# Moving the last two query casts later and cutting them in quarters, with a fourth pair of strips

## The chip, the cores and the metric

The kernel runs on one core of one Trainium2 chip. The core has five instruction queues that run side by side and wait for each other through semaphores: PE (TensorE, matrix products and transposes; its weight loads are shown as PEld), DVE (VectorE), ACT (ScalarE), POOL (GpSimd) and SP (SyncE, which here only issues transfers). Transfers are carried out by 16 DMA engines; a transfer issued on SP's queue appears as q1 in the profile, one issued on POOL's queue as q0.

The metric is the device time of one launch in microseconds (us). The kernel before took 377.2 us in the median of three runs (375.63 to 378.17). Its profile is that of another execution, which took 375.06 us.

## The reference, cut to what matters

Two parts follow each other. The first is attention whose keys and values are one small projected table per batch; the second sends each row of its result through two of eight small adapters.

```python
B, N, C = q.shape                      # 4, 12288, 128
kv_pool = kv.reshape(B, H//4, 4, W//4, 4, C).mean(axis=(2, 4))
k = v = kv_pool.reshape(B, -1, C) @ w_sr          # 768 rows a batch
a = softmax(q @ k.T / sqrt(C))                    # 12288 x 768 a batch
x = (a @ v).reshape(B * N, C)                     # 49152 rows
logits = x @ w_gate                               # 8 experts
w = softmax of the two largest logits
out = x + sum over those two e of w_e * (x @ A[e]) @ B[e]     # rank 16
```

## The kernel before, in words

The 49152 rows are cut into 96 chunks of 512 rows (`T`), numbered k = 0 to 95; four chunks make a query group g of 2048 rows (`GT`), 24 groups in all, six to a batch. The main loop has one slot per chunk number. In slot k the scores of a later chunk are computed (`scores`: PE tile `sg`, exponentials on ACT into `em`), chunk k-1 is attended (`attend`: PE tile `acc`), and older chunks go through the adapter steps: `normalize` (DVE, `xn`), a transposition of `xn`, `down` (PE, `h_ps`), `gate` (DVE, multiplies `h_ps` by the gates `gw`), a transposition of the gated activations, `up` (PE, `d_ps`), `finish` (DVE, `osb`) and a store of `osb` to the output. `route` and `gates` work out the gates on POOL. The order on each engine is the order in which the loop records the operations; nothing reorders them.

**Queries.** Groups 2 and up come in two steps. `cast_q` (L79 to L84) issues on POOL's queue a transfer from the float32 queries to a bf16 buffer in device memory, `qbf`, laid out in 16 rows of eight pieces of 2048 elements. `load_qT` and `part_qT` (L86 to L92) later issue on SP's queue a transposing transfer from `qbf` to the tile `qT`. The tables `casts` and `loads` (L492 to L496) say in which slot: the casts of groups 4 to 23 stand in slots 8, 12, 15, 18 and so on to 66, always first in the slot (`begin`); the loads of the last groups stand in slots 61, 64, 67, 74, 78, 82 and 86. From slot 72 on a load is cut in two halves, two slots apart. Groups 0 and 1 are loaded as float32 (`load_q`, L109) and transposed by PE instead; their eight tiles `qf` are taken from the pool of `osb`.

**Transpositions by transfer.** In slots 13 to 69 about three gated chunks in four are transposed by a transfer: `gate_turn` writes the gated activations into one half of a strip `hs` and a transfer on SP's queue turns it into a strip `ht`; two chunks share one pair of strips. There are three `hs` and four `ht`, used in turn, so that a gate that opens a new pair waits until the transfers from the pair three before it have landed. The chunk goes through `up` six slots after its gate. From slot 70 on, another form is used: `narrow` (L415, POOL) writes the normalized chunk of the slot as bf16 into a strip `turn`, `gate` writes the gated chunk beside it, and one transfer (`turn_dma`, L419) turns both. Chunks 68 to 89 (`by_dma`) have their normalized rows turned so; the product `h_ps` of slot k+2 reads what the transfer of slot k has brought.

**SP's queue** issues in program order: loads of kv rows, stores, `ht` transfers, `qT` loads, `turn` transfers. One that cannot be issued yet holds those behind it.

**The output pool** `opool` has six buffers `osb`; the one that writes the seventh waits until the store from the first has landed.

The lines that the steps below touch, in `begin` and `gate_turn`:

```python
if k in casts:
    cast_q(4 + casts.index(k))
...
sheets.append([hpool.tile([P, 2, S, P], BF16, tag=tag, name=tag, bufs=n)
               for tag, n in (("hs", 3), ("ht", 4))])
```

Of the kernel before, what the change touches and what calls it, by code (L numbers as in the profile page):

```python
# [10 lines left out]
FP32 = mybir.dt.float32  # L11
BF16 = mybir.dt.bfloat16
# [8 lines left out]
def kernel(  # L21
# [10 lines left out]
    nc = tc.nc  # L32
    P = 128
    B, N, C = q.tensor.shape
# [5 lines left out]
    S = T // P  # L40
    GC = 4
    GT = GC * T
# [15 lines left out]
    gpool = ctx.enter_context(tc.tile_pool(name="gpool", bufs=6))  # L58
    run = ctx.enter_context(tc.tile_pool(name="run", bufs=3))
    hpool = ctx.enter_context(tc.tile_pool(name="hpool", bufs=4))  # L60
    opool = ctx.enter_context(tc.tile_pool(name="opool", bufs=6))
    qdram = ctx.enter_context(tc.tile_pool(name="qdram", bufs=1, space=bass.MemoryType.DRAM))
    ps_s = ctx.enter_context(tc.tile_pool(name="ps_s", bufs=2, space=bass.MemoryType.PSUM))
    ps_a = ctx.enter_context(tc.tile_pool(name="ps_a", bufs=1, space=bass.MemoryType.PSUM))
# [2 lines left out]
    keep = tc.keep_in_program_order  # L67
# [8 lines left out]
    NG = N // GT  # L76
    q_bf, qT, kvr, spare = {}, {}, {}, {}

    def cast_q(g):  # L79
        t = qdram.tile([16, GT // 16 * C], BF16, tag=f"q{g}", name=f"qbf{g}")  # L80
        src = q[g // NG, (g % NG) * GT:(g % NG + 1) * GT]
        keep(nc.gpsimd.dma_start(t.rearrange("r (u x) -> r u x", u=8),
                                 src.rearrange("(u r x) c -> r u (x c)", r=16, u=8)))
        q_bf[g] = t  # L84

    def load_qT(g):  # L86
        qT[g] = qpool.tile([P, GT], BF16, tag="qT", name="qT")
# [7 lines left out]
    def load_kv(b, h, r, x):  # L95

        if (b, h) not in kvr:
            kvr[b, h] = kvpool.tile([P, 4, 2, 4 * C], FP32, tag="kvr", name="kvr")
        rows = H // 3
        src = kv[b, h * rows + r:(h + 1) * rows:4].rearrange("y (w k) c -> y w (k c)", k=8)  # L100
        if x is None:
            keep(nc.sync.dma_start(kvr[b, h][:, r].rearrange("p g c -> p (g c)"), src))
        else:
            keep(nc.sync.dma_start(kvr[b, h][:, r, x], src[:, :, x * 4 * C:(x + 1) * 4 * C]))


    q_f = {}

    def load_q(g, m):  # L109
        q_f[g, m] = opool.tile([P, S, C], FP32, tag="osb", name="qf")  # L110
        src = q[0, g * GT:(g + 1) * GT].rearrange("(p j) c -> p j c", p=P)
        keep(nc.sync.dma_start(q_f[g, m], src[:, m * S:(m + 1) * S]))

# [44 lines left out]
    for m in range(GC):  # L158
        load_q(0, m)
    load_first(1)  # L160
    load_first(2)
    for m in range(GC):
        load_q(1, m)
# [174 lines left out]
    SOLO, TURN = NCHUNK - 6, NCHUNK - 28  # L338
# [91 lines left out]
    def gate(k, into=None):  # L430
        k0, m = first[k], k - first[k]
        hg[k] = run.tile([P, S, P], BF16, tag="hg", name="hg") if into is None else into
        keep(nc.vector.tensor_tensor(  # L433
            hg[k].rearrange("p s (e r) -> p (s e) r", e=E),
            hp[k].rearrange("p s (e r) -> p (s e) r", e=E),
            gw[k0][:, m * S:(m + 1) * S].rearrange("p s e -> p (s e)")
            .unsqueeze(2).broadcast_to([P, S * E, RK]), op=ALU.mult))

    sheets, turns = [], []

    def gate_turn(k, alone):
        i = len(turns) % 2
        if i == 0:
            sheets.append([hpool.tile([P, 2, S, P], BF16, tag=tag, name=tag, bufs=n)
                           for tag, n in (("hs", 3), ("ht", 4))])
        src, dst = sheets[-1]
        gate(k, src[:, i])
        hgT[k] = dst[:, i]
        turns.append(k)
        if alone or i == 1:  # L450
            lo = i if alone else 0
            keep(nc.sync.dma_start(dst[:, lo:i + 1].rearrange("c h s p -> c (h s) p"),
                                   src[:, lo:i + 1].rearrange("p h s c -> p (h s c)"), transpose=True))
# [26 lines left out]
    def cast_first():  # L480
        keep(nc.gpsimd.tensor_copy(late, q_f[1, 2][:, 0, 0:1]))
        for g in (2, 3):
            cast_q(g)
        for g in (2, 3):
            load_qT(g)
# [5 lines left out]
        scores(k, r)  # L491

    sums, rest = [], []
    casts = [8, 12] + [15 + 3 * i for i in range(18)]
    loads = {4 * g - 6: g for g in range(4, B * NG) if not 17 <= g <= 19}
    loads.update({61: 17, 64: 18, 67: 19})  # L496
    assert len(casts) == B * NG - 4

    rows_at, adds_at = {}, {}
    for b in range(2, B):  # L500
        for n in range(12):
            h, r, t = n // 4, n % 4, b * NB - 33 + 2 * n
# [15 lines left out]
    def begin(k):  # L518
        nonlocal sums, rest
        b, i = divmod(k, NB)  # L520
        g = k // GC
        if k in casts:
            cast_q(4 + casts.index(k))
        if k in rows_at:
            load_kv(*rows_at[k], None)
        if i == 0 and 0 < b < B - 1:
            rest = prepare(b + 1, nc.gpsimd)[1]
        if k == 3:
            sums, rest = prepare(1, nc.gpsimd)
            sums = sum(sums, [])  # L530
        if 3 <= k < 15:
            load_kv(1, (k - 3) // 4, (k - 3) % 4, None)
        if k == 7:
            for _ in range(2):
                sums.pop(0)()
# [11 lines left out]
    enter, t, left = {}, 1, list(range(NCHUNK - 3))  # L547
# [14 lines left out]
    def step(op, *w):  # L562
        v = [int(x) if x.isdigit() else engines.get(x, pools.get(x)) for x in w]
        if op == "T":
            turn_rows(v[0], 2 * (v[2] // 2) if w[1] == "s" else v[2],
                      v[2] % 2 if w[1] == "s" else v[3])
        elif op == "turn":
            turn_q(v[0] // GC, v[0] % GC, *v[1:])
        elif op in ("keys", "keys2", "values"):
            first_rest[v[0]][("keys", "keys2", "values").index(op)]()  # L570
        elif op == "gates":
            later.pop(0)()
        else:
            {"spin": spin, "proj1": project, "proj2": project2, "sum": add_rows, "sc": unit,
             "late": cast_first, "cast": cast_weights, "slot": begin, "at": attend, "atp": attend_part,
             "norm": normalize, "top": top, "route": route, "tr": transposes, "down": down,
             "gate": gate, "up": up, "fin": finish}[op](*v)
# [23 lines left out]
    for k in range(k1, NCHUNK):  # L601
        b, i = divmod(k, NB)
        ka = att.get(k, [])
        kx = enter.get(k, [])
        begin(k)

        def after_norm(kn):
# [86 lines left out]
        for x_ in kx[:1]:  # L694
            if x_ in by_queue:
                gate_turn(x_, x_ < 59 or x_ == TURN - 3)
                late_up[k + 6] = [x_]
                if k in loads:
                    load_qT(loads[k])
            elif x_ in by_strip:  # L700
                gate(x_, strip(k, 0)[:, 1])
                turn_dma(k, *todo, (hgT, x_))
                todo = []
            else:
                gate(x_)
# [200 lines left out]
```

## Time and profile before

| what | us |
|---|---|
| median of three runs | 377.2 |
| the profiled execution | 375.06 |
| its span, first to last instruction | 373.2 |
| PE busy (96% of the span) | 359.1 |
| ACT busy (79%) | 295.2 |
| DVE busy (78%) | 291.3 |
| POOL busy (58%) | 218.2 |
| DMA, q1 (SP's queue), share of 16 engines | 78.2% |
| DMA, q0 (POOL's queue: the casts), share of 16 engines | 18.2% |

A row of the timeline gives start, duration, engine, line, operation, out<-in, shapes and count; brackets behind it give how long the engine had been idle and what ended that. SP's rows are durations of issuing; when the data lands is told apart from that ("DMA to landing"). A wait is put down to the semaphore that moved last, so where the engine named had long been done the true releaser was another one, often a transfer. The shares of the queues are sums over packets, each from its start to its end, and can pass 100%.

### The profile page before, as it was taken

Reading aid. Unit: us, or ns where it says so; the run is one execution under the profiler, and the core shown is the slowest. Engines: PE = TensorE matmul, PEld = TensorE weight load, DVE = VectorE, ACT = ScalarE, POOL = GpSimd, SP = SyncE. Lnnn points to the kernel's source line nnn. Section 1 sums busy time; section 2 is a strip of 40 time slices with the busy share of each in tenths; the row PEclk is TensorE's granted clock in tenths of the full one; section 3 lists DMA queues with packets and bytes.
Section 4 is the critical chain, followed back from the end, with each engine's and each line's share of the span. In section 5 each row is a group of like instructions: output and inputs, shape, how many; then the busy total and the mean of one; then the engine's idle time right before and its main releaser. Section 6 shows DMA issues by size and latency. Waiting matters only on the chain.

```text
span 373.2 us, 11208 instructions
## 1 busy us (share of the span) xinstructions
PE 359.1 (96%) x4254; PEld 280.5 (75%) x4260; DVE 291.3 (78%) x924; ACT 295.2 (79%) x368; POOL 218.2 (58%) x493
## 2 busy tenths in 40 slices
PE   8799999999999999999999999999898999999993
PEld 5577778877787787787787777777676777777782
DVE  1446789887888888888888898888687877777785
ACT  1448986777778888888888888878777999999873
POOL 0120368888766566667657657658454666666452
PEclk9999999999999999999999999999999999999998
DMA  7989669999999999999899999999999999999523
GB/s 250 383 289 227 227 162 295 287 255 241 200 249 321 262 245 227 275 265 290 223 237 217 229 264 249 308 230 223 238 235 191 257 201 222 201 222 201 142 89 141
DMA packets 77222, 88.36 MB, mean 237 GB/s; under 512 B 53584, under 2 KB 54352, under 8 KB 76752
## 3 DMA queue, kind: packets, MB, share of 16 engines
q1 hardware_dynamic: 73568, 75.91, 78.2%
q0 software_dynamic: 3168, 11.54, 18.2%
q8 instruction: 33, 0.54, 0.6%
q10 hardware_dynamic: 432, 0.20, 0.2%
q14 instruction: 21, 0.17, 0.1%
HBM read 50.53 MB, written 36.70 MB: 234 GB/s over the span
## 4 chain that ended last, share of the span: by engine, by line
PE 85%; DMA 6%; DVE 3%; ACT 2%; POOL 1%; issue 1%; SPq 0%; ACTq 0%; POOLq 0%; DVEq 0%
PE acc L70 34%; PE sg L70 30%; PE h_ps L70 5%; PE tt_ps L70 5%; PE d_ps L70 5%; DMA kvr<-in_kv_dram 4%; PE kpT_ps L70 2%; DMA turn<-turn 2%; PE v_ps L70 1%; ACT em L303 1%; DVE xn L332 1%; DVE kvr L135 1%; POOL kvr L221 1%; DMA out_dram<-osb 1%; PE kfT_ps L70 1%
## 5 line engine op out<-in xcount | busy, mean ns | idle before, releaser
L303 ACT ACTIVATE em<-sg 128x1024 f16<-128x1024 f32 x288 | 284.2, 1022 | 59.4 <-PE sg L70 53.0
L70 PE MATMUL sg<-qT,kfT 128*128 128x512 bf16 x570 | 169.5, 379 | 1.0 <-ACT em L303 0.7
L70 PE MATMUL acc<-vx,em 128*128 128x136 f16 x2280 | 167.2, 223 | 0.6 <-DVE xn L332 0.5
L70 PEld LDWEIGHTS <-em 128*128 128x128 f16 x2304 | 146.7, 98 | 18.2 <-DVE xn L332 2.4
L332 DVE TENSOR_TENSOR xn<-acc,rinv 128x540 f32<-128x540 f32 x95 | 68.4, 720 | 3.3
L466 DVE TENSOR_TENSOR osb<-d_ps,xn 128x512 f32<-128x512 f32 x91 | 62.1, 687 | 1.8
L364 POOL TENSOR_TENSOR over<-xn,srt 128x64 f32<-128x64 f32 (+1 forms) x120 | 30.9, 278 | 49.7 <-DVE srt L352 49.7
L516 POOL TENSOR_TENSOR kvr<-kvr 128x512 f32<-128x512 f32 (+1 forms) x48 | 57.0, 1202 | 0.5
L70 PEld LDWEIGHTS <-kfT 128*128 128x128 bf16 x576 | 45.1, 98 | 2.7 <-issue 1.0
L379 POOL TENSOR_TENSOR gw<-th,over 128x64 f32<-128x64 f32 (+1 forms) x60 | 17.3, 289 | 50.8 <-ACT th L377 48.6
L324 DVE RECIPROCAL rinv<-acc 128x4 f32<-128x4 f32 x95 | 17.3, 182 | 37.5 <-PE acc L70 35.0
L433 DVE TENSOR_TENSOR hs<-h_ps,gw 128x512 bf16<-128x512 f32 x45 | 30.6, 679 | 7.5 <-POOL gw L380 4.9
L401 DVE COPY tts<-tt_ps 128x512 bf16<-128x512 bf16 (+1 forms) x72 | 35.8, 497 | 0.0
L70 PEld LDWEIGHTS <-xn 128*128 128x128 bf16 x296 | 22.5, 98 | 16.7 <-DVE xn L332 0.4
L352 DVE MAX8 srt<-xn 128x8 f32<-128x8 f32 x380 | 34.4, 152 | 0.1
L70 PEld LDWEIGHTS <-tts 128*128 128x128 bf16 x376 | 26.1, 98 | 5.9 <-DVE tts L401 0.2
L70 PE MATMUL h_ps<-a_bf,tts 128*128 128x128 bf16 x284 | 27.5, 219 | 0.0
L70 PE MATMUL tt_ps<-id_bf,xn 128*128 128x128 bf16 x284 | 27.4, 219 | 0.0
L70 PEld LDWEIGHTS <-turn 128*128 128x128 bf16 x184 | 13.8, 98 | 12.9 <-DMA turn<-turn 3.6
L370 POOL TENSOR_SCALAR over<-over 128x64 f32<-128x64 f32 (+1 forms) x60 | 19.8, 331 | 5.3
L223 POOL TENSOR_TENSOR kvr<-kvr 128x512 f32<-128x512 f32 x18 | 22.4, 1270 | 0.1
L70 PEld LDWEIGHTS <-ht 128*128 128x128 bf16 x180 | 13.8, 98 | 10.9 <-issue 0.7
(96 smaller groups left out, 295.9 us busy)
## 6 DMA issues: line engine op xcount, KB each, us to landing
out_dram<-osb SPq DMA_DIRECT2D x94, 256.0 KB, 4.8
kvr<-in_kv_dram SPq DMA_DIRECT2D x45, 512.0 KB, 6.7
qbf<-in_q_dram POOLq DMA_DIRECT2D x22, 512.0 KB, 7.2
qf<-in_q_dram SPq DMA_DIRECT2D x8, 256.0 KB, 7.6
kvr<-in_kv_dram SPq DMA_DIRECT2D x6, 256.0 KB, 7.7
ht<-hs SPq DMA_TRANSPOSE x42, 6.4
qT<-qbf SPq DMA_TRANSPOSE x26, 7.7
out_dram<-osb SPq DMA_DIRECT2D x3, 128.0 KB, 2.3
```

The source lines that it names most:

```text
L70: return keep(nc.tensor.matmul(*a, **k))
L223: keep(adder.tensor_tensor(u[:, lo:hi], u[:, lo:hi], v[:, lo:hi], op=ALU.add))
L303: keep(nc.scalar.activation(o, i_, AF.Exp, bias=0.0, scale=scale))
L324: keep(nc.vector.reciprocal(ri, acc[k][:, :, VC]))
L332: keep(nc.vector.tensor_tensor(x[:, :, 0:VC], acc[k][:, :, 0:VC], ri.unsqueeze(2).broadcast_to([P, S, VC]), op=ALU.mult))
L352: keep(nc.vector.max(srt[k0][:, m, s], xn[k][:, s, C:C + E]))
L364: keep(eng.tensor_tensor(d, lg, so[:, :, i].unsqueeze(2).broadcast_to([P, n, 8]), op=ALU.subtract))
L370: keep(eng.tensor_scalar(mask, mask, 0.0, None, op0=ALU.is_ge))
L401: keep(nc.vector.tensor_copy(sb[:, lo:hi], ps[:, lo:hi]))
L433: keep(nc.vector.tensor_tensor(hg[k].rearrange("p s (e r) -> p (s e) r", e=E), hp[k].rearrange("p s (e r) -> p (s e) r", e=E), gw[k0][:, m ...
L466: keep(nc.vector.tensor_tensor(osb, dp[k], xn[k][:, :, 0:C], op=ALU.add))
L516: keep(nc.gpsimd.tensor_tensor(u, u, v, op=ALU.add))
```

## The change

Four things change.

1. The casts of groups 22 and 23 leave slots 63 and 66. Each is cut in four by rows of `qbf` (rows 0 to 3, 4 to 7, 8 to 11, 12 to 15); the quarters of group 22 stand first in slots 72, 73, 74 and 75, those of group 23 in slots 78, 79, 80 and 81. A whole cast reads 16 x 8 pieces of 2048 elements, a quarter 4 x 8.
2. The strips `hs` become four, as the strips `ht` are.
3. The four `qf` tiles of group 1 are taken from the strips `ht`, reread as float32, not from the pool of `osb`.
4. The pool of `osb` has five buffers instead of six.

```diff
-    opool = ctx.enter_context(tc.tile_pool(name="opool", bufs=6))
+    opool = ctx.enter_context(tc.tile_pool(name="opool", bufs=5))
...
-    def cast_q(g):
-        t = qdram.tile([16, GT // 16 * C], BF16, tag=f"q{g}", name=f"qbf{g}")
+    def cast_q(g, lo=0, hi=16):
+        if lo == 0:
+            q_bf[g] = qdram.tile([16, GT // 16 * C], BF16, tag=f"q{g}", name=f"qbf{g}")
         src = q[g // NG, (g % NG) * GT:(g % NG + 1) * GT]
-        keep(nc.gpsimd.dma_start(t.rearrange("r (u x) -> r u x", u=8),
-                                 src.rearrange("(u r x) c -> r u (x c)", r=16, u=8)))
-        q_bf[g] = t
+        keep(nc.gpsimd.dma_start(q_bf[g].rearrange("r (u x) -> r u x", u=8)[lo:hi],
+                                 src.rearrange("(u r x) c -> r u (x c)", r=16, u=8)[lo:hi]))
...
     def load_q(g, m):
-        q_f[g, m] = opool.tile([P, S, C], FP32, tag="osb", name="qf")
+        if g:
+            t = hpool.tile([P, 2, S, P], BF16, tag="ht", name="qf")
+            q_f[g, m] = t.rearrange("p h s c -> p (h s c)").bitcast(FP32).rearrange("p (s c) -> p s c", s=S)
+        else:
+            q_f[g, m] = opool.tile([P, S, C], FP32, tag="osb", name="qf")
...
-            sheets.append([hpool.tile([P, 2, S, P], BF16, tag=tag, name=tag, bufs=n)
-                           for tag, n in (("hs", 3), ("ht", 4))])
+            sheets.append([hpool.tile([P, 2, S, P], BF16, tag=tag, name=tag)
+                           for tag in ("hs", "ht")])
...
-    casts = [8, 12] + [15 + 3 * i for i in range(18)]
+    casts = [8, 12] + [15 + 3 * i for i in range(16)]
+    quarters = {TURN + 4 + 6 * n + i: (B * NG - 2 + n, 4 * i) for n in range(2) for i in range(4)}
...
         if k in casts:
             cast_q(4 + casts.index(k))
+        if k in quarters:
+            g, r = quarters[k]
+            cast_q(g, r, r + 4)
```

More of the change, by code (lines that the diff above doesn't have):

```diff
@@ L493 @@
     sums, rest = [], []
-    casts = [8, 12] + [15 + 3 * i for i in range(18)]
+    casts = [8, 12] + [15 + 3 * i for i in range(16)]
+    quarters = {TURN + 4 + 6 * n + i: (B * NG - 2 + n, 4 * i) for n in range(2) for i in range(4)}
     loads = {4 * g - 6: g for g in range(4, B * NG) if not 17 <= g <= 19}
     loads.update({61: 17, 64: 18, 67: 19})
-    assert len(casts) == B * NG - 4
+    assert len(casts) == B * NG - 6
     rows_at, adds_at = {}, {}
```

## The prediction

> **What bounds the kernel now.** I read the busy shares, then the table of stretches, to see where PE loses time.
>
> ```profile
> PE 359.1 (96%) x4254; PEld 280.5 (75%) x4260; DVE 291.3 (78%) x924; ACT 295.2 (79%) x368; POOL 218.2 (58%) x493
> ```
> ```profile
> 250.00:260.00 10.00, 10.00 (x123) 7.70 (x122) 7.84 (x26) 8.73 (x11) 6.61 (x13) 1.00 1.16 227
> 260.00:270.00 10.00, 8.79 (x106) 6.65 (x105) 7.09 (x22) 7.25 (x10) 5.44 (x10) 1.00 1.07 232
> 270.00:280.00 10.00, 9.88 (x118) 7.58 (x114) 8.40 (x30) 7.66 (x11) 5.40 (x18) 1.00 1.06 233
> 280.00:290.00 10.00, 8.59 (x106) 6.77 (x107) 7.44 (x21) 7.72 (x11) 5.03 (x17) 1.00 0.89 190
> ```
>
> PE is busy 96% of the span, and a stretch in which it is full gives nothing back. In these rows (start and end, length, then busy time of PE, PEld, DVE, ACT and POOL) PE has a hole of 1.21 us in 260 to 270 and of 1.53 in 270 to 290. The timeline says what made them.
>
> ```profile
> 261.93 0.36 DVE L352 MAX8 srt<-xn 128x8 f32<-128x8 f32 x4
> 264.45 0.69 DVE L433 TENSOR_TENSOR hs<-h_ps,gw 128x512 bf16<-128x512 f32 x1 [2.16 <-PE sg L70]
> 265.19 0.38 PE L70 MATMUL d_ps<-b_bf,ht 128*128 128x128 bf16 x4 [0.75 <-DVE hs L433]
> 266.04 0.53 PE L70 MATMUL acc<-vx,em 128*128 128x136 f16 x6 [0.47 <-DVE xn L332]
> ```
> ```profile
> 281.41 0.40 PE L70 MATMUL h_ps<-a_bf,turn 128*128 128x128 bf16 x4 [1.53 <-DMA turn<-turn]
> ```
>
> The first hole is a gate on DVE that stood idle for 2.16 us before it wrote `hs`. PE `sg` is named as its releaser, but this gate (chunk 63) reads no scores; it opens a new pair of strips, and with three pairs it needs the one of chunks 57 and 58 back. PE waits for the gate (0.75) and then for the late `xn` behind it (0.47). The second hole, 1.53 us before 281.41, stands ahead of the first product that reads a `turn` strip.
>
> ```profile
> 246.74 1.22 SPq L452 DMA_TRANSPOSE ht<-hs  x1
> 247.61 0.60 POOL L82 DMA_DIRECT2D qbf<-in_q_dram  x1
> 256.96 0.60 POOL L82 DMA_DIRECT2D qbf<-in_q_dram  x1
> 250.65 6.51 SPq L92 DMA_TRANSPOSE qT<-qbf  x1
> 257.87 1.54 SPq L452 DMA_TRANSPOSE ht<-hs  x1
> 261.65 5.42 SPq L92 DMA_TRANSPOSE qT<-qbf  x1
> 270.45 2.72 SPq L92 DMA_TRANSPOSE qT<-qbf  x1
> 274.82 0.69 DVE L433 TENSOR_TENSOR turn<-h_ps,gw 128x512 bf16<-128x512 f32 x1 [0.55 <-POOL gw L380]
> 278.23 1.29 SPq L419 DMA_TRANSPOSE turn<-turn  x1
> ```
>
> Both holes come from SP's queue running late. The two `qT` loads issued beside the casts of slots 63 and 66 took 6.51 and 5.42 us to issue, the next one, with no cast, 2.72. Chunk 58's transfer stood behind the first of them and was issued at 257.87. The first `turn` strip was written at 275.51, its transfer issued only at 278.23.
>
> What a cast does to the other queue stands in the DMA view: the stretch of the cast at 256.96 (rows q0 and q1: packets, MB, share of 16 engines), then a stretch with none.
>
> ```profile
> q0 software_dynamic: 144, 0.52, 57.0%
> q1 hardware_dynamic: 652, 0.39, 23.2%
> ```
> ```profile
> q1 hardware_dynamic: 4899, 2.57, 107.7%
> ```
>
> 57.0% of the 6.7 us from 256.9 to 263.6 is 3.8 us of each engine for the cast; meanwhile SP's queue falls to 23.2%, against 107.7% from 301 to 313. The landings agree: the `ht` transfer of 257.87 (first row below), and that of 276.28 with no cast near.
>
> ```profile
> DMA to landing us min/median/max: 6.5/6.5/6.5
> ```
> ```profile
> DMA to landing us min/median/max: 3.1/3.1/3.1
> ```
>
> So a whole cast adds up to 3.4 us to a transfer beside it.
>
> **The change part by part.** *Casts leave slots 63 and 66.* The two `qT` loads fall towards 2.72 us, which gives SP back (6.51 - 2.72) + (5.42 - 2.72) = 6.5 us, more than the 2.7 us by which the first `turn` transfer was late. Issued at 275.5 and landing 3.1 later it is there at 278.6, before the 279.88 at which PE wanted it: gain 1.53.
>
> *Fourth pair.* Chunk 63's gate then needs the pair before that of 57 and 58, whose last transfer is that of 246.74; and with SP earlier chunk 58's transfer lands earlier as well, which matters, since the product at 265.19 reads it. Gain 0.75 + 0.47 = 1.22. Together 2.75, all that PE loses between 250 and 290. The other gates hide their waits in slack already; DVE finds nothing later behind it.
>
> *Five output buffers.* This is the page's row of the stores (KB each, median us to landing):
>
> ```profile
> out_dram<-osb SPq DMA_DIRECT2D x94, 256.0 KB, 4.8
> ```
>
> One `osb` is written a slot, and a slot is 3.2 us or more (304.81 to 307.98 below), so five buffers leave about 16 us for a store that lands in 4.8: nothing. In the tail the last write reuses, instead of the buffer of chunk 91's store, that of chunk 92's, issued at 367.64:
>
> ```profile
> 367.64 2.60 SPq L462 DMA_DIRECT2D out_dram<-osb  x5
> 369.46 0.42 DVE L776 TENSOR_TENSOR osb<-tail_ps,xn 128x256 f32<-128x256 f32 x1 [0.36 <-PE tail_ps L70]
> ```
> ```profile
> DMA to landing us min/median/max: 2.0/2.0/2.0
> ```
>
> It lands at 369.66, the write began at 369.46: loss 0.2 on the path that ends the kernel. The end of the run hangs on this write and its store, so nothing hides it.
>
> *First loads.* Two of the `qf` tiles of group 1 no longer wait until PE has read those of group 0. SP's list of waits has this for them:
>
> ```profile
> SPq L112 <- DMA kvr<-in_kv_dram: 2.2, 4, 0.9
> ```
>
> They waited for kv transfers, not for PE, and that order stays: zero.
>
> *Quarters on POOL.* Each costs 0.60 us of issue (the rows above), eight of them 4.8. In their slots POOL has this gap:
>
> ```profile
> 301.62 0.29 POOL L370 TENSOR_SCALAR over<-over 128x32 f32<-128x32 f32 x1
> 302.43 0.61 POOL L415 CAST turn<-xn 128x512 bf16<-128x512 f32 x1 [0.52 <-DVE xn L332]
> ```
>
> The quarter stands between these two: 301.91 + 0.60 = 302.51, so `narrow` is 0.1 late at most, and its transfer, issued at 303.26, still finds it done at 303.12. Zero; up to 0.1 a slot if that cover goes.
>
> *Quarters beside the `turn` transfers.* This decides the sign. The transfer of slot k needs the gate of slot k, and the product `h_ps` of slot k+2 needs the transfer: a loop over two slots.
>
> ```profile
> 303.26 1.30 SPq L419 DMA_TRANSPOSE turn<-turn  x1
> 306.93 1.52 SPq L419 DMA_TRANSPOSE turn<-turn  x1
> 304.81 0.39 PE L70 MATMUL h_ps<-a_bf,turn 128*128 128x128 bf16 x4
> 307.98 0.39 PE L70 MATMUL h_ps<-a_bf,turn 128*128 128x128 bf16 x4
> 311.42 0.40 PE L70 MATMUL h_ps<-a_bf,turn 128*128 128x128 bf16 x4
> DMA to landing us min/median/max: 3.4/4.1/4.4
> ```
> ```profile
> 286.22 2.24 SPq L419 DMA_TRANSPOSE turn<-turn  x1
> 291.82 0.39 PE L70 MATMUL h_ps<-a_bf,turn 128*128 128x128 bf16 x4
> DMA to landing us min/median/max: 3.5/3.6/3.8
> ```
>
> The landing rows are for the four transfers of 301 to 311, slots 77 to 80, and the three of 286 to 294, slots 73 to 75. In slots 78 and 79 there lie 4.72 and 4.49 us between issue and product, mean 4.6; less the median landing of 4.1 the slack is 0.5. In slots 72 to 75, where PE does more per slot, it is 5.6 - 3.6 = 2.0. A delay d that lasts stretches two slots by d less the slack, one slot by half of that.
>
> No row shows a quarter, so d has two ends. Spread over all 16 engines like a whole cast, a quarter takes 3.8 / 4 = 0.95 us of each: d is at most 0.95. But only 4 rows of 8 pieces are read now instead of 16; if the 16 rows were what filled the 16 engines, four engines get what each got from a whole cast, 3.8 us, and a transfer that uses all engines lands when the slowest is done. A slot is 3.2 us, so the delay saturates there: d = 3.2. I take 2.0, the middle, because the two ends are equally near to the one kind of row there is. Slots 78 to 81 then cost 4 x (2.0 - 0.5) / 2 = 3.0, slots 72 to 75 nothing.
>
> The sum: -2.75 + 0.2 + 3.0 = +0.45 us. On its own execution 375.06 becomes 375.5; the median of the runs is 2.1 above that execution, so I carry the difference over: 377.2 becomes 377.6, no change.
>
> [...]
>
> **The rivals.** *The quarters spread evenly* (faster). d = 0.95 costs 4 x 0.45 / 2 = 0.9: -2.75 + 0.2 + 0.9 = -1.65, 375.5; with no cost at all 374.6. For it: 16 engines carry every transfer seen. Against: those had 16 or more outer rows.
>
> *Each quarter holds four engines as long as a whole cast held all* (slower). d = 3.2 costs 4 x 2.7 / 2 = 5.4 in slots 78 to 81 and 4 x 1.2 / 2 = 2.4 in slots 72 to 75: +7.8 + 0.2 - 2.75 = +5.25, 382.4. It outweighs the gain from d = 1.8 and passes 1% from d = 2.8. For it: the 3.4 us that a whole cast added to a transfer. Against: slots that get longer move the transfers away from the next quarter.
>
> *The change does not do what it says*: SP stays late from its kv loads and stores alone, and the first `turn` transfer with it. Only the 1.22 comes: +2.0, 379.2. Against: the 2.72 row.
>
> **How the numbers follow.** Forecast 0.38 (376.4 to 379), even spread 0.30, slower rival 0.20, SP still late 0.12. Below 374.6 and above 382.4 I leave about one in ten each. A difference under 1%, 3.8 us, is about what a measurement of this kernel cannot tell from no change. Faster by over 1% would need more than the 2.75 there is to gain: 0.05. Slower by over 1% is the slower rival: 0.20. The rest, 0.75, lies within.
>
> **What would show it.** After the change the gate of chunk 63 has no idle time before it and PE no hole between 260 and 282, with `qT` loads near 2.7 us; if they still take 5, the first step is wrong. In slots 78 to 81 the waits of PE `h_ps` for `turn` give 2(d - 0.5) in total; none means an even spread, about 5 us the slower rival. Holes in slots 72 to 75 speak for d over 2. The last write of `osb` follows a landing by under 0.1. A stall at a place that is full today would make all of it wrong.

## The result, and the profile after

The changed kernel takes **388.1 us** in the median of four runs (385.25 to 395.72), the kernel before, in the same rounds, 376.4. The ratio is 1.031, 95% interval 1.026 to 1.036: slower by 3%. Disturbed executions (here the one of 395.72) are left out of every ratio in this text, but not out of the medians, so a ratio can differ from the quotient of two medians. The forecast was 377.6, its range ended at 382.4, and the slower rival was priced at 382.4 too. The profiled execution took 388.04 us, with a span of 386.3 against 373.2.

The page's row of the busy shares, for the kernel after:

```profile
PE 364.4 (94%) x4260; PEld 283.2 (73%) x4260; DVE 292.3 (76%) x924; ACT 295.8 (77%) x368; POOL 222.3 (58%) x499
```

It splits the 13.1 us of longer span in two. PE is idle for 386.3 - 364.4 = 21.9 us where it was 373.2 - 359.1 = 14.1: 7.8 more. And it is *busy* for 5.3 us more, though it has the same work to do. So there are two things to find, waits and slower work. The table of stretches after, to be read beside that in the prediction (start and end, length, busy time of PE, PEld, DVE, ACT and POOL, the granted clock of PE, DMA share, GB/s):

```profile
260.00:270.00 10.00, 10.00 (x127) 7.88 (x125) 8.43 (x28) 8.70 (x11) 6.94 (x12) 1.00 1.15 251
270.00:280.00 10.00, 10.00 (x120) 7.72 (x117) 8.41 (x30) 7.78 (x10) 5.27 (x18) 1.00 0.77 184
280.00:290.00 10.00, 9.48 (x116) 7.24 (x116) 8.51 (x24) 8.33 (x11) 7.27 (x21) 1.00 1.06 142
290.00:300.00 10.00, 8.04 (x95) 5.63 (x92) 6.15 (x23) 7.40 (x9) 5.78 (x19) 1.00 1.46 208
300.00:310.00 10.00, 6.71 (x63) 5.20 (x63) 4.38 (x14) 4.96 (x7) 3.72 (x11) 0.83 0.85 208
310.00:320.00 10.00, 7.85 (x91) 5.63 (x89) 5.96 (x22) 8.54 (x12) 8.23 (x25) 1.00 1.17 131
320.00:330.00 10.00, 8.21 (x71) 6.39 (x72) 4.04 (x14) 4.37 (x6) 2.37 (x9) 0.66 1.06 185
```

From 260 to 280, where the kernel before had its holes, PE is now full: both gains came. Then it has holes from 280 to 330, and in two rows the granted clock is 0.83 and 0.66, where every row of before that was shown has 1.00. The timeline of PE names the holes:

```profile
222.01 0.27 PE L70 MATMUL kfT_ps<-id_bf,vb 128*128 128x128 bf16 x2 [1.17 <-DVE osb L470]
280.06 0.40 PE L70 MATMUL h_ps<-a_bf,turn 128*128 128x128 bf16 x4
287.60 0.40 PE L70 MATMUL h_ps<-a_bf,turn 128*128 128x128 bf16 x4 [0.48 <-DMA turn<-turn]
292.12 0.40 PE L70 MATMUL h_ps<-a_bf,turn 128*128 128x128 bf16 x4 [0.96 <-DMA turn<-turn]
296.67 0.40 PE L70 MATMUL h_ps<-a_bf,turn 128*128 128x128 bf16 x4 [1.00 <-DMA turn<-turn]
303.30 0.61 PE L70 MATMUL h_ps<-a_bf,turn 128*128 128x128 bf16 x4 [3.29 <-DMA turn<-turn]
314.72 0.40 PE L70 MATMUL h_ps<-a_bf,turn 128*128 128x128 bf16 x4 [0.21 <-DMA turn<-turn]
321.79 0.61 PE L70 MATMUL h_ps<-a_bf,turn 128*128 128x128 bf16 x4 [3.74 <-DMA turn<-turn]
```

The first `turn` product (280.06) has no bracket any more; before it had 1.53. The six later brackets make 9.68 us of waits for `turn`. The row at 222.01 is a new hole of 1.17, far ahead of the quarters, behind a write of `osb`. With the 2.87 us of holes that are gone (0.75, 0.47, 1.53 and a wait of 0.12 before): 9.68 + 1.17 - 2.87 = 7.98, beside the 7.8 of the page. That accounts for the waits.

The slower work shows in the same rows. Behind the two longest waits four products take 0.61 us in place of 0.40. Shorter stretches of the table, after:

```profile
304.00:305.00 1.00, 1.00 (x7) 0.60 (x6) 0.69 (x1) 0.20 (x1) 0.00 (x0) 0.50 1.87 500
324.00:326.00 2.00, 2.00 (x15) 1.45 (x13) 0.69 (x5) 0.38 (x2) 0.99 (x4) 0.50 1.53 187
```

The granted clock is 0.50 here. The trace's record of that clock has it at 0.5 for 3.41 us from 303.14 and for 6.83 us from 320.21. PE is busy for 8.5 of these 10.24 us, with 59 products, 6.9 a us; in the stretch from 260 to 280, at 1.00, it is 243 in 20.00 us, 12.2 a us. Half of the 8.5 put down to the clock is some 4.2 us, an estimate; by the products a us it would be 3.6. The other 1.1 of the 5.3, beside the 4.2, isn't located. Three kernels below with the changed pools and no such stretch have 0.8 to 1.0 more busy time than before as well (360.1, 360.0 and 359.9). No part of the prediction had the lower clock.

Why the `turn` transfers are late: the landing rows after, for the four issued from 281.4 to 296.7 (beside the quarters of group 22) and for the four from 309.4 to 324.6 (group 23), which were 3.5/3.6/3.8 and 3.4/4.1/4.4 near there before:

```profile
DMA to landing us min/median/max: 6.1/6.7/7.5
```
```profile
DMA to landing us min/median/max: 4.8/6.4/10.6
```

And the issues of the casts in the page after, whole ones and quarters (KB each, median us to landing):

```profile
qbf<-in_q_dram POOLq DMA_DIRECT2D x20, 512.0 KB, 7.8
qbf<-in_q_dram POOLq DMA_DIRECT2D x8, 128.0 KB, 7.9
```

A quarter carries a quarter of the bytes and lands no sooner than a whole cast. The DMA view from 280 to 287, where POOL's queue has one quarter's packets, says why:

```profile
q1 hardware_dynamic: 2176, 0.63, 83.7%
q0 software_dynamic: 144, 0.13, 16.0%
```

The whole cast of before had 144 packets as well. Of these 144, in the trace's list of packets, 32 carry 4096 bytes and 112 carry 4 bytes. The 32 run from 281.77 to 286.15, 4.38 us, and take 17.1 us together: 3.9 at a time on average. At the shortest in these traces, the 32 of a quarter take 2.46 us (10.4 together, 4.2 at a time), and the 128 of a whole cast 2.49 (41.4 together, 16.6 at a time). The list names no engine, so that a quarter by rows sits on four of them isn't shown beyond these counts.

What this does to SP's queue shows in the DMA view from 283.4 to 285.8, inside that quarter. It has this row and none for q1:

```profile
q0 software_dynamic: 24, 0.10, 21.9%
```

So no packet of SP's queue starts in these 2.4 us. In the list of packets 15 of its packets, 256 bytes each, stand open all the while. They started before 283.4 and end together at 286.3, right behind the quarter's last. Each took some 3.1 us; the median of such packets before, from 301 to 313, is 0.02. The `turn` transfer issued at 281.43 lands at 287.56, and PE's next wait ends with it. From the second quarter of a group on, its data packets start late too, 3.4 to 6.2 us after the issue (1.5 to 1.7 for the first); what they wait for isn't shown.

SP's queue after is late again, in a new place:

```profile
261.36 2.48 SPq L92 DMA_TRANSPOSE qT<-qbf  x1
268.28 2.71 SPq L92 DMA_TRANSPOSE qT<-qbf  x1
291.26 4.22 SPq L92 DMA_TRANSPOSE qT<-qbf  x1
296.69 1.32 SPq L423 DMA_TRANSPOSE turn<-turn  x1
319.86 3.99 SPq L92 DMA_TRANSPOSE qT<-qbf  x1
```

The loads that lost their casts take 2.48 and 2.71 us to issue, as forecast. But of the halves of `qT` loads that now have a quarter beside them, those shown take 4.22 and 3.99, where the halves of before took 1.16 to 2.22. The transfer at 296.69 stood behind the first of these (its strip was written by 293.29), and it is the one that PE waits 3.29 us for.

### The profile page after: what moved, and what is told of

Its sections match the earlier page's. It is cut to its first block, busy times and chain, and to the rows that moved or that the text cites. A ratio compares the mean times of both kernels' runs of the same rounds, so it can differ in the third digit from the quotient of the medians.

```text
span 386.3 us, 11218 instructions
## 1 busy us (share of the span) xinstructions
PE 364.4 (94%) x4260; PEld 283.2 (73%) x4260; DVE 292.3 (76%) x924; ACT 295.8 (77%) x368; POOL 222.3 (58%) x499
## 3 DMA queue, kind: packets, MB, share of 16 engines
q0 software_dynamic: 4032, 11.54, 17.0%
## 4 chain that ended last, share of the span: by engine, by line
PE 79%; DMA 11%; DVE 4%; POOL 2%; ACT 1%; issue 1%; SPq 0%; DVEq 0%; ACTq 0%; POOLq 0%
PE acc L70 32%; PE sg L70 28%; DMA turn<-turn 5%; PE h_ps L70 5%; PE tt_ps L70 5%; PE d_ps L70 5%; DMA kvr<-in_kv_dram 4%; DMA out_dram<-osb 2%; PE kpT_ps L70 2%; PE v_ps L70 1%; DVE xn L336 1%; DVE osb L470 1%; ACT em L307 1%; DVE kvr L139 1%; PE kfT_ps L70 1%
## 5 line engine op out<-in xcount | busy, mean ns | idle before, releaser
L70 PE MATMUL sg<-qT,kfT 128*128 128x512 bf16 x576 | 172.2, 382 | 0.8 <-ACT em L307 0.7
L70 PE MATMUL acc<-vx,em 128*128 128x136 f16 x2280 | 169.2, 224 | 0.0
L70 PEld LDWEIGHTS <-em 128*128 128x128 f16 x2304 | 148.6, 99 | 17.9 <-DVE xn L336 1.7
L70 PEld LDWEIGHTS <-turn 128*128 128x128 bf16 x184 | 14.1, 101 | 22.9 <-DMA turn<-turn 13.9
L437 DVE TENSOR_TENSOR turn<-h_ps,gw 128x512 bf16<-128x512 f32 x24 | 16.4, 684 | 11.0 <-PE h_ps L70 10.5
```

The lines of the kernel that those rows point to most:

```text
L70: return keep(nc.tensor.matmul(*a, **k))
L437: keep(nc.vector.tensor_tensor(hg[k].rearrange("p s (e r) -> p (s e) r", e=E), hp[k].rearrange("p s (e r) -> p (s e) r", e=E), gw[k0][:, m ...
```

## The experiments

All times in us. "Waits" are the idle times of PE at `turn` products from 270 to 330 in the profiled execution; "at 0.5" is how long the granted clock was 0.5 in that execution, without its last 12 us, where the kernels before and after have such a stretch too (5.37 and 6.63 us). The ratio is to the kernel before in the same rounds. That kernel itself lay between 371.7 and 382.6 there.

| kernel | median | before | ratio, 95% interval | waits | at 0.5 |
|---|---|---|---|---|---|
| after | 388.1 | 376.4 | 1.031 (1.026 to 1.036) | 9.7 | 3.41 + 6.83 |
| quarters alone | 387.9 | 375.4 | 1.031 (1.025 to 1.037) | 11.1 | 3.41 + 6.83 |
| pools alone | 378.1 | 375.4 | 0.994 (0.988 to 1.001) | 2.0 | none |
| after, without the two casts | 374.9 | 375.4 | 1.002 (0.998 to 1.005) | 0.6 | none |
| before, without the two casts | 373.6 | 377.6 | 0.997 (0.993 to 1.002) | none | none |
| after, quarters by pieces | 378.6 | 375.4 | 1.005 (1.001 to 1.010) | 6.1 | none |
| before, quarters by pieces (second run) | 378.2 | 377.7 | 1.003 (0.986 to 1.019) | 5.9 | none |
| whole casts in slots 72 and 78 | 379.4 | 377.6 | 1.017 (1.003 to 1.030) | 7.8 | 6.83 |
| early casts, one set of quarters | 379.9 | 376.4 | 1.008 (1.004 to 1.012) | 6.6 | 3.41 |
| after, with fill | 388.0 | 377.6 | 1.036 (1.021 to 1.050) | 8.5 | none |
| early casts (5 rounds) | 373.6 | 376.4 | 0.993 (0.990 to 0.995) | 0.8 | none |

### Which part loses: quarters alone, pools alone

The quarters by rows, with six `osb`, three `hs` and the first loads as before:

```diff
-    opool = ctx.enter_context(tc.tile_pool(name="opool", bufs=5))
+    opool = ctx.enter_context(tc.tile_pool(name="opool", bufs=6))
...
-            sheets.append([hpool.tile([P, 2, S, P], BF16, tag=tag, name=tag)
-                           for tag in ("hs", "ht")])
+            sheets.append([hpool.tile([P, 2, S, P], BF16, tag=tag, name=tag, bufs=n)
+                           for tag, n in (("hs", 3), ("ht", 4))])
```

> Only the casts are changed (quarters by rows in slots 72 to 81), the pools are those of before. Theory (the quarters are nearly all of the loss): 385 to 388 us, turn waits of 8 us or more and some 10 us of granted clock at 0.5. Rival (quarters and the smaller output pool lose together, stores being held by the quarters): 381 us or less.

387.9 us, ratio 1.031. Its timeline has the waits of the changed kernel over again:

```profile
286.81 0.40 PE L70 MATMUL h_ps<-a_bf,turn 128*128 128x128 bf16 x4 [1.23 <-DMA turn<-turn]
292.12 0.40 PE L70 MATMUL h_ps<-a_bf,turn 128*128 128x128 bf16 x4 [1.75 <-DMA turn<-turn]
298.91 0.40 PE L70 MATMUL h_ps<-a_bf,turn 128*128 128x128 bf16 x4 [3.23 <-DMA turn<-turn]
314.88 0.40 PE L70 MATMUL h_ps<-a_bf,turn 128*128 128x128 bf16 x4 [1.50 <-DMA turn<-turn]
321.56 0.61 PE L70 MATMUL h_ps<-a_bf,turn 128*128 128x128 bf16 x4 [3.34 <-DMA turn<-turn]
```

The quarters alone make the whole loss: the ratio is that of the changed kernel. The hole at 222 isn't there, so that one belongs to the five `osb`.

The pools alone, with whole casts in slots 63 and 66:

```diff
-    casts = [8, 12] + [15 + 3 * i for i in range(16)]
-    quarters = {TURN + 4 + 6 * n + i: (B * NG - 2 + n, 4 * i) for n in range(2) for i in range(4)}
+    casts = [8, 12] + [15 + 3 * i for i in range(18)]
+    quarters = {}
```

> Only the pools are changed (four hs, five osb, qf of group 1 in ht); the casts stand whole in slots 63 and 66 as before. Theory (the fourth hs gives back the 1.2 us of the late gate, five osb lose about 1.2 us at a store that lands late while SP's queue is behind): 375 to 378 us, no change. Rival (five output buffers are a main part of the loss): 380 us or more, with waits of DVE osb for stores of 3 us or more.

The ratio, 0.994 (0.988 to 1.001), can't be told from no change; it rests on three of ten executions, and the median of all ten is 378.1. The profiled one took 379.97. Four of its seven holes (6.9 us in all), from the timeline of PE:

```profile
221.96 0.27 PE L70 MATMUL kfT_ps<-id_bf,vb 128*128 128x128 bf16 x2 [1.13 <-DVE osb L470]
257.39 0.40 PE L70 MATMUL d_ps<-b_bf,ht 128*128 128x128 bf16 x4 [0.71 <-DMA ht<-hs]
270.27 0.40 PE L70 MATMUL d_ps<-b_bf,ht 128*128 128x128 bf16 x4 [1.33 <-DMA ht<-hs]
285.91 0.40 PE L70 MATMUL h_ps<-a_bf,turn 128*128 128x128 bf16 x4 [1.57 <-DMA turn<-turn]
```

With the casts where they were, a fourth pair frees the gate of chunk 63, and PE then waits for the late `ht` transfers themselves. So the strip wasn't the cause of the hole; SP's late queue was, which the next runs bear out with three strips. The wait behind `osb` is there again.

### What taking the casts away is worth

Here the two casts are left out, once with the changed pools, once with those of before:

```diff
-        keep(nc.sync.dma_start(t[:, lo:hi], q_bf[g][:, lo * C:hi * C], transpose=True))
+        keep(nc.sync.dma_start(t[:, lo:hi], q_bf[min(g, 21)][:, lo * C:hi * C], transpose=True))
...
-    quarters = {TURN + 4 + 6 * n + i: (B * NG - 2 + n, 4 * i) for n in range(2) for i in range(4)}
+    quarters = {}
```

> The changed kernel with the eight quarters left out; the last two groups are loaded from group 21's cast instead (so the queries of the last two groups are not the right ones; all other work is the same). Theory (removing the casts from slots 63 and 66 is worth the 2.75 us of PE holes, less about 1.2 us at five output buffers): 374 to 376 us, no turn wait. Rival (SP's queue stays late from kv loads and stores alone): the first turn wait of 1.5 us stays, 376 to 378 us.

> The kernel before without the casts of groups 22 and 23; these two groups are loaded from the cast of group 21, so the queries of the last two groups are not theirs. It has six osb and three strips hs. Theory: the hole of 1.53 us at the first turn strip goes, the hole at the gate of chunk 63 goes in part or whole since chunk 58's transfer is on time, and no stall at osb comes in, as it did with five buffers: 372.6 to 373.9 against 375.4. Rival (the two casts cost nothing net where they stand): 375.4, as without them and with the changed pools (ratio 1.0015).

With the pools of before no idle time over 0.1 us is left on PE between 200 and 350, neither at the gate of chunk 63 nor at the first `turn` strip. Two rows of its table of stretches:

```profile
260.00:280.00 20.00, 20.00 (x246) 15.86 (x244) 17.29 (x53) 16.67 (x21) 11.54 (x30) 1.00 0.86 204
280.00:300.00 20.00, 20.00 (x242) 15.47 (x240) 16.31 (x54) 18.11 (x25) 12.45 (x42) 1.00 1.00 219
```

So the 2.75 us were really there to gain, with three strips as well as with four. The median, 373.6 (371.6 to 376.62), is in the range expected; the ratio, 0.997 (0.993 to 1.002), is no proof of it.

With the changed pools the median is 374.9, and the profiled execution has this in PE's timeline:

```profile
207.67 0.38 PE L70 MATMUL tt_ps<-id_bf,xn 128*128 128x128 bf16 x4 [0.40 <-DVE osb L470]
214.72 0.38 PE L70 MATMUL tt_ps<-id_bf,xn 128*128 128x128 bf16 x4 [2.64 <-DVE osb L470]
```

DVE waited 4.31 us there for a store of `osb` to land before it could write that buffer again. The hole at 222.01 in the changed kernel is of the same kind:

```profile
207.55 7.67 SPq L92 DMA_TRANSPOSE qT<-qbf  x1
215.32 0.53 SPq L466 DMA_DIRECT2D out_dram<-osb  x1
221.27 0.69 DVE L470 TENSOR_TENSOR osb<-d_ps,xn 128x512 f32<-128x512 f32 x1 [1.36 <-DMA out_dram<-osb]
```

The write at 221.27 waited for the store issued at 215.32, which landed at 221.18. By the order of writes and stores, that buffer had been full since 202.41. Its store spent 12.9 us in line on SP's queue, 7.67 of them behind a `qT` load, and 5.9 in flight. With six buffers the write would have needed the store before, which landed at 215.20, and would not have waited. The lack of the sixth buffer costs 0.8 to 3 us of PE's time in the traces with five, up to all that the change had to gain.

### How much is the shape: quarters by pieces

The same quarters cut along the other dimension, so that each has 16 outer rows of two pieces:

```diff
-        keep(nc.gpsimd.dma_start(q_bf[g].rearrange("r (u x) -> r u x", u=8)[lo:hi],
-                                 src.rearrange("(u r x) c -> r u (x c)", r=16, u=8)[lo:hi]))
+        keep(nc.gpsimd.dma_start(q_bf[g].rearrange("r (u x) -> r u x", u=8)[:, lo // 2:hi // 2],
+                                 src.rearrange("(u r x) c -> r u (x c)", r=16, u=8)[:, lo // 2:hi // 2]))
```

First with the changed pools:

> The changed kernel, but each quarter takes two of the eight pieces of all 16 rows instead of all pieces of four rows: same bytes, same slots, same number of transfers on POOL's queue. Theory (a quarter by rows sits on four engines, eight packets each, and holds every turn transfer until they are through; the PE stalls then halve the granted clock): with 16 outer rows a quarter is two packets on each of 16 engines, about 1 us; no turn wait over 1 us, no clock at 0.5 before the tail, 374 to 378 us. Rival (any cast in these slots costs that much, by its presence on the other queue or its issue on POOL): 385 us or more, the turn waits of about 9 us stay.

378.6 us in place of 388.1, no clock at 0.5 before the tail: the rival falls. The theory was too hopeful as well, with waits up to 1.88 us where it allowed 1, and 378.6 where it ended at 378. Then with the pools of before. The profiled execution of the first such run had a granted clock of 0.56 from end to end (621.7 us), so its waits say nothing; its ten times gave a median of 377.4 and a ratio of 1.002 (0.998 to 1.007), and the kernel was run again for a trace.

> The quarters cut by pieces, so that each has 16 outer rows, with the pools of before (six osb, three strips hs). Theory (quarters that use all 16 engines still cost the turn transfers some 6 us, as with the changed pools; the rest of what was seen there, 1.46 us, was the fifth osb): that hole goes, the holes of slots 63 to 70 stay away, turn stalls of about 5 to 6 us in sum, none over 3, no granted clock of 0.5 before the tail; 0 to 1 % above the kernel before. Rival (spread quarters are free beside turn transfers and the changed pools made the stalls): no turn stall over 0.3 us, 371.6 to 373, as without the two casts.

> Again the quarters cut by pieces with the pools of before, for a trace at full clock (the execution profiled before ran at 0.56 from end to end and its waits say nothing). Theory (quarters on all 16 engines still delay the turn transfers): turn stalls of 4 to 6 us in sum, no idle time at osb, no 0.5 before the tail, 375 to 380. Rival (only the changed pools made the stalls seen with these quarters): no turn stall over 0.3 us, 371.6 to 373.6.

The waits in the trace of the second run:

```profile
290.73 0.40 PE L70 MATMUL h_ps<-a_bf,turn 128*128 128x128 bf16 x4 [1.86 <-DMA turn<-turn]
294.62 0.40 PE L70 MATMUL h_ps<-a_bf,turn 128*128 128x128 bf16 x4 [0.33 <-DMA turn<-turn]
299.50 0.40 PE L70 MATMUL h_ps<-a_bf,turn 128*128 128x128 bf16 x4 [1.54 <-DMA turn<-turn]
```

With 2.15 more at 314.47 that is 5.88 us, within the 4 to 6 expected; the rival (only the pools made these waits) falls. Two rows of its page, PE's busy share and the landing of the quarters:

```profile
PE 359.4 (95%) x4254; PEld 280.4 (74%) x4260; DVE 291.7 (77%) x924; ACT 295.5 (78%) x368; POOL 221.5 (59%) x499
qbf<-in_q_dram POOLq DMA_DIRECT2D x8, 128.0 KB, 4.5
```

A quarter lands after 4.5 us here and after 7.9 by rows, the same 32 packets of 4096 bytes in both. Here those of the first quarter are through in 1.77 us, with 18.7 us of packet time: 10.6 at a time. So the shape is worth 387.9 - 377.4, some 10 us. But spread quarters don't come free: their waits eat the gain, and a ratio of 1.002 (0.998 to 1.007) is no change. And PE is busy for 359.4, nearly as before (359.1): there is no stretch at 0.5.

### Place or cut: whole casts in slots 72 and 78

```diff
-    casts = [8, 12] + [15 + 3 * i for i in range(18)]
+    casts = [8, 12] + [15 + 3 * i for i in range(16)] + [TURN + 4, TURN + 10]
```

> The kernel before with the casts of groups 22 and 23 whole in slots 72 and 78. A whole cast takes 3.8 us of each of 16 engines and added up to 3.4 us to a transfer. Theory (what hurts is that each quarter costs the transfers beside it as much as a whole cast): two delays in place of eight, 3.4 less the slack of 2.0 in slot 72 and 3.4 less 0.5 in slot 78 makes at most 4.3 us, less the 2.0 to 2.8 us that slots 63 and 66 get back: 376 to 378 against 375.4 for the kernel before, turn stalls 4.3 in sum at most and none over 3 us. Rival (any cast bytes beside the turn transfers cost by their amount, so the place is at fault and not the cut): as slow as the quarters by pieces or slower, 378.6 to 388.

379.4 us, above the 376 to 378 of the theory and in the rival's span. The sum of the waits, 7.8, is above the 4.3 at most, and most of it is in two places:

```profile
286.83 0.40 PE L70 MATMUL h_ps<-a_bf,turn 128*128 128x128 bf16 x4 [1.23 <-DMA turn<-turn]
309.69 0.61 PE L70 MATMUL h_ps<-a_bf,turn 128*128 128x128 bf16 x4 [5.82 <-DMA turn<-turn]
```

In slot 72 a whole cast cost 1.23, near the 1.4 worked out. In slot 78 the transfer beside the cast landed 9.56 us after its issue, not 3.4 later than usual but more than 5, and the next one 8.91. So one cast among these transfers can cost several us, whole or cut; the place is at fault, and the cut by rows multiplies it: eight quarters by rows made more waits (11.1) and lost more than two whole casts.

### Do the slots with more slack hold: one set of quarters

Early casts (below), but group 22 in quarters by rows in slots 72 to 75:

```diff
-    casts = [8, 12] + [15 + 3 * i for i in range(18)]
+    casts = [8, 12] + [15 + 45 * i // 17 for i in range(17)]
+    quarters = {TURN + 4 + i: (B * NG - 2, 4 * i) for i in range(4)}
...
+            cast_q(g_ if g_ < B * NG - 2 else B * NG - 1)
```

> The kernel with the early casts, but group 22 is cast in quarters by rows in slots 72 to 75, and group 23 takes its place in slot 57; pools of before. Theory (a quarter by rows delays a turn transfer by 3 us or more, which passes the slack of 2.0 us in these slots too): turn stalls of 4 to 7 us in sum at chunks 70 to 73, with the clock at 0.5 if one is over 3 us, 376 to 380. Rival (the slack of 2.0 covers these slots, and only the quarters of slots 78 to 81 cost): no turn stall over 0.5 us, 371.6 to 373.5.

379.9 us; the waits are 1.65, 1.75 and 3.18, in sum 6.6, all at the quarters of group 22. The rival falls: the slack of 2.0 us didn't cover slots 72 to 75. Against the kernel with early casts alone (373.6) these four quarters cost 6.3 us.

### Why the clock fell

The changed kernel, with PE kept at work inside the two longest waits:

```diff
+        for n in range(S * fill.get(k, 0)):
+            s = n % S
+            mm(hp[k][:, s], b_bf, a_bf, start=(s == 0), stop=(s == S - 1))
...
+    fill = {73: 4, 77: 4}
```

> The changed kernel with one thing added: ahead of the h_ps products of chunks 73 and 77, the two that stood idle for 3.29 and 3.74 us, PE does 16 more products of the same size into the same tile, which the real ones then overwrite. By the row of four (0.39 us) they take 1.57 us in each place and lie inside the wait. Theory (PE idle for over 3 us brings the granted clock down to 0.5): the longest idle time falls to about 1.7 and 2.2 us, no entry of 0.5 is left before the tail, and the time falls by the 4.3 us that the halved clock cost, to about 384. Rival (the clock falls for another reason, the transfers or the load on the chip): the entries of 0.5 stay and the time stays at 388. Where the long stalls fall on other chunks in an execution, the fill costs up to 3.1 us and tells less.

The profiled execution did as the theory said: no entry of 0.5 before the tail, 384.25 us. The other three took 387.8 to 388.3, with a mean granted clock of 0.983 to 0.988 against its 0.993. They have no trace; which waits they had stays open, and the median, 388.0, doesn't bear the theory out. The 16 products themselves took 1.06 us, not 1.57. So the question was put in another way, with no cast and no late transfer near, in the kernel with early casts:

```diff
+        for _ in range(hold.get(k, 0)):
+            keep(nc.vector.memset(hp[k], 0.0))
...
+    hold = {70: 4, 76: 7, 82: 10}
```

> The kernel with the early casts, which has no hole in PE before the tail, with three holes put in: before the h_ps products of chunks 70, 76 and 82, DVE writes that tile 4, 7 and 10 times with zeros, which the products wait for and then overwrite. At 0.4 to 0.7 us each, by the row of the gate (0.69 for the same tile), PE is idle for some 2, 4 and 6 us, with no cast and no late transfer near. Theory (idle time of PE over about 3 us halves the granted clock for a while): none after the first hole; an entry of 0.5, 3.41 or 6.83 us long, at the third, and at the second if its idle time is over 3.3. Rival (the clock fell for the load on the transfers): no entry of 0.5 before the tail.

PE's timeline, and then the table of the stretches behind each hole:

```profile
288.68 0.38 PE L70 MATMUL h_ps<-a_bf,turn 128*128 128x128 bf16 x4 [1.85 <-DVE rinv L324]
311.95 0.38 PE L70 MATMUL h_ps<-a_bf,turn 128*128 128x128 bf16 x4 [3.50 <-DVE rinv L324]
338.25 0.59 PE L70 MATMUL h_ps<-a_bf,turn 128*128 128x128 bf16 x4 [5.50 <-DVE rinv L324]
```
```profile
288.70:292.00 3.30, 3.30 (x42) 2.66 (x43) 2.80 (x9) 1.83 (x2) 1.54 (x5) 1.00 0.50 146
312.30:315.70 3.40, 3.40 (x23) 2.37 (x21) 1.98 (x7) 1.02 (x1) 1.99 (x7) 0.50 0.34 66
338.30:343.00 4.70, 4.70 (x32) 3.60 (x32) 2.29 (x7) 1.66 (x2) 2.08 (x7) 0.50 0.42 59
```

After 1.85 us of idle time the clock stays at 1.00 (42 products in 3.3 us); after 3.50 it is 0.50 for 3.41 us (23 products in 3.4), after 5.50 for 6.83. In this one execution idle time of PE lowered its clock with no cast beside it; the rival falls. The price: its span is 386.9 against 371.8 with early casts alone; the four holes (with 1.08 at the first `turn`, less the 0.84 that stands there without them) make 11.1 of those 15.1, and some 4 us are left for the 10.24 us at 0.5.

### A version that beats both: the casts earlier

If casts beside late stretches of SP's queue are what costs, they can be put where nothing is tight. The kernel before with one line changed, so that the last casts stand in slots 57 and 60:

```diff
-    casts = [8, 12] + [15 + 3 * i for i in range(18)]
+    casts = [8, 12] + [15 + 45 * i // 17 for i in range(18)]
```

> The kernel before with the 18 casts of groups 6 to 23 spread over slots 15 to 60 in place of 15 to 66, so that none stands in slots 61 to 69. Theory (both holes of the kernel before, 2.75 us in all, come from the casts of slots 63 and 66 beside SP's late queue): both go without anything taking their place, 372.6 to 373.5 against 375.4. Rival (SP's queue is as late with the casts 15% denser, only in other slots): 375 to 377, with new holes at waits for ht or for the strips hs between slots 40 and 62.

> Again the kernel before with the casts of groups 6 to 23 spread over slots 15 to 60, in more rounds: 371.6 to 373.5 us. Theory: with both holes gone it is faster than the kernel before by the 2.9 us that those held, ratio about 0.992, and its runs lie closer together than those of before. Rival (the gain seen was chance): a ratio whose interval holds 1.

In the first run the median is 372.9, with no idle time over 0.1 us on PE between 200 and 350, but a ratio of 0.996 (0.992 to 1.0002); in the second, with more rounds, 373.6 (372.31 to 374.48) and 0.993 (0.990 to 0.995). It is faster than both kernels, by 0.7% over before, and its runs lie closer together. In the trace of the second run a wait of 0.5 for a `qT` is left between 180 and 200, and 0.84 us at the first `turn` strip:

```profile
279.92 0.40 PE L70 MATMUL h_ps<-a_bf,turn 128*128 128x128 bf16 x4 [0.84 <-DMA turn<-turn]
```

## Why the prediction was wrong

**What bounds the kernel, and the gain of 2.75: right.** Both holes are gone after the change, with `qT` loads of 2.48 and 2.71 us to issue where 2.72 was forecast, and the gate of chunk 63 has no idle time before it. One reason was half wrong: the fourth pair was credited with 1.22. Without the two casts that hole closes with three strips too, and with the fourth pair but the casts in place it turns into waits for `ht`. The 1.22 belonged to SP's queue as well.

**Five buffers in steady slots, "nothing": wrong by 1.2.** "16 us for a store that lands in 4.8" counted a store from its issue and left out the line on SP's queue ahead of it: 12.9 us for the store behind the hole at 222.01, 18.8 from full buffer to landing. The trace of before had it to read: a buffer full at 205.74 has its store issued at 214.36 and landed at 222.84, 17.1 us in all. In the tail, on the other hand, the 0.2 didn't come from there: the last write of `osb` began at 382.75, 0.19 after the store in question had landed, and it was PE's product that ended its idle time (0.52, before 0.36).

**First loads and POOL: right.** The waits of these loads are still for kv transfers (2.3 us, before 2.2). The quarters take 0.64 to 0.66 us each on POOL between the rows named; no wait of PE goes back to them.

**Quarters beside the `turn` transfers: the step that failed.** It had the upper end of d as a rival, but took 2.0, "the middle", and priced slots 78 to 81 at 3.0 us and slots 72 to 75 at nothing. The waits were 3.95 (0.21 and 3.74) and 5.73 (0.48, 0.96, 1.00 and 3.29). The 3.95 lies near the 3.0 by luck: it is one long wait, not four equal ones. Three things were mis-sized:

- d itself. In slots 72 to 75 the landing went from 3.6 to 6.7, d = 3.1: the rival's end; in slots 78 to 81 from 4.1 to 6.4, d = 2.3, with single landings up to 10.6. The trace of before couldn't decide between the ends: its casts all have 16 outer rows. Each end had a reason, the middle had none, so the upper one deserved more than 0.20 against 0.38.
- What stands between the transfers. The loop counted a transfer's flight against its slack and left SP's queue out. Halves of `qT` loads lie in the same slots (74, 76, 78 and so on) and took 4.22 and 3.99 us to issue beside quarters, as those in 63 and 66 had. The late queue had been read there, in the prediction's own rows, as the cause of the holes; it was moved, not removed. So the first set, to which the rival gave 2.4, lost 5.73, of which 3.29 at the transfer that stood behind such a half, and the waits came to 9.7 in place of the rival's 7.8.
- Saturation. "The delay saturates" at 3.2: a transfer after the change landed 10.6 us after its issue, one beside a whole cast 9.56.

The even-spread rival failed too: spread quarters should have cost 0.9 and cost 5.9 us of waits. Its d of 0.95 shared out the bytes alone. What else a spread quarter costs, the queue or the engines, these runs didn't separate.

**Not in any case: the clock.** The slower rival spread its 7.8 us over eight slots, 1.4 at most in each. That the delay would gather in single waits of 3.29 and 3.74, with products at a granted clock of 0.5 behind them, no outcome had. It cost some 4.2 us by the estimate above, nearly the whole distance (4.8) from the forecast to the slower rival.

**The sum with what was measured:** -2.87 for the holes that went, +9.68 at `turn`, +1.17 at `osb`, +4.2, the estimate, for the clock: +12.2, beside the span's +13.1. The rest lies in the busy time that wasn't located.

## What to carry to other kernels

Before you cut a transfer into parts, look at how many outer rows each part keeps. Here parts with 4 in place of 16 took as long as the whole, which the row of landings shows at once (128 KB in 7.9 us, 512 KB in 7.8); parts that kept all 16 were worth some 10 us against that, and still gained nothing over the uncut casts in their old place. When a transfer moves to another place, price it there against everything that the neighbouring queue issues in those slots, not only against the transfer whose slack you worked out; first look for a place where nothing waits, as the earlier slots were here. And a wait of PE had a second price here once it passed some 3 us: none up to 2.64 us was followed by a lower clock, each from 3.18 us on by 3.41 or 6.83 us at 0.5.

## What the runs showed that was not expected

**The granted clock and idle time.** Over the traces here (but the one at 0.56), between the start and the tail, no idle time of PE up to 2.64 us was followed by a lower clock; from 3.18 us on each was, at 0.5, for 3.41 us or twice that, 6.83:

| idle, us | kernel | at 0.5, us |
|---|---|---|
| 1.85 | holes put in | none |
| 2.29 | after, with fill | none |
| 2.64 | after, without the two casts | none |
| 3.18 | one set of quarters | 3.41 |
| 3.23 | quarters alone | 3.41 |
| 3.29 | after | 3.41 |
| 3.34 | quarters alone | 6.83 |
| 3.50 | holes put in | 3.41 |
| 3.74 | after | 6.83 |
| 5.50 | holes put in | 6.83 |
| 5.82 | whole casts | 6.83 |

The order isn't strict: 3.34 gave 6.83 and 3.50 gave 3.41. What decides between the two lengths isn't shown, nor what idle times between 2.64 and 3.18 us would do.

**Packets of a quarter.** A quarter by rows brings 112 packets of 4 bytes beside its 32 of 4096; by pieces it is 16 beside the same 32. The page's q0 row for eight quarters and twenty whole casts counts 4032 packets in the kernel after.
